# Another table of places for the loads, scatters and first expert loads of an attention with experts behind it

## The chip, the cores and the metric

The kernel runs on one core of a Trainium2 chip. The metric is the time of one execution in device microseconds, the median of several runs. TensorE is called PE, VectorE DVE, ScalarE ACT, GpSimd POOL and SyncE SP.

## The reference

Eight batches of eight heads, 576 positions, head size 64. Half of the heads see a local window of 32 positions, the other half the positions of the same remainder modulo 32. The heads' outputs are the tokens of a mixture of eight experts, of which each token takes one.

```python
scores = scale * np.matmul(q, k.transpose(0, 1, 3, 2))
masks = np.stack([mask_local if h < H // 2 else mask_strided for h in range(H)], axis=0)
scores = np.where(masks[None, :, :, :], scores, -1000000000.0)
attn = softmax(scores)
x = (attn @ v).transpose(0, 2, 1, 3).reshape(B * S, H * D)
...
logits = x @ w_gate + modality_bias[modality_id]
e_idx = np.argmax(logits, axis=1)
...
h = np.maximum(x[mask] @ w1[e], 0.0)
out[mask] = gate_w[mask, None] * (h @ w2[e])
```

(`softmax(scores)` stands for the reference's maximum, exponential and division.)

## The kernel before, in words

The attention is cut into 32 units, taken alternately from the local heads (class `Local`, L356 on) and the strided heads (class `Strided`, L459 on); each works on two batches or two heads at once. Four batch pairs, `bp` 0 to 3, have eight units each. A unit has five stages: its two loads of queries and keys (a and b, each 64 partitions, L354), its values (v and w, L371 and L473; a strided unit has v alone), `masks` (L379, L478), `scores` (`s` at L391 and L398, `ss` at L485, with the maximum, the subtraction and the exponential on DVE and ACT), `turn` (the transposes `t` and `ts`, L236) and `values` (`o` at L439 and L447, `oa` at L535, `ob` at L542, whose results DVE or ACT writes to the tokens `xa`, `xb` and `xc`). The main loop over n, 0 to 34, interleaves them: scores of unit n, turn of unit n-2, masks of unit n+1, values of unit n-3. Between them stand five places: 0 ahead of the scores, 1 behind them, 2 behind turn, 3 behind masks, 4 behind values. PE runs exactly in the order in which this code is written; on the other engines a scheduler orders what isn't pinned.

`FETCH[(n, place)]` names the loads that are issued at a place, as "20a" for unit 20, part a. All loads are issued by SP, in order, and each gets a wait on the last PE instruction written ahead of it:

```python
def paced(ins):
    behind(ins, next(i for i in reversed(nc.cur_bb.bb.instructions) if i.engine == mybir.EngineType.PE).name)
```

`SPOTS[n]` names the places at which `slot(n, place)` issues one further thing: a scatter of 128 finished tokens to their expert's region in DRAM (`xd`, L680, issued by POOL, nine for each batch pair), or, when the scatters of the first two pairs have been issued, the next step of `early()` (L1143 on; ten steps): the first expert's weights (`raw` in halves, then `lqk`, which serves as weight buffer again, L902) and the first two blocks of its tokens (`fx` in halves, L861). For n of 32 and up a missing entry means places 1, 2 and 4.

```python
def slot(n, place):

    if place not in SPOTS.get(n, (1, 2, 4) if n >= nu else ()):
        return
    if calm and not (todo and todo[0].args[0] < NBP - 2):
        next(calm[0], None)
        ...
    else:
        scatter_rows(1)
```

When a pair's units are done, `finish_pair` and `route` (L556 and L606 on) turn its tokens both ways, compute the gate (`lg`), the expert of each token and its row there. The rows of a pair are `posi` (L677, DVE), which the scatters read; one buffer is used for all pairs, so `posi` of a pair waits until the scatters of the pair before have landed. The token loads `fx` of the first expert wait for all scatters of the first two pairs (`collected`, L307 on). `turn_tokens` transposes these tokens on PE (`xt`, L236) behind the last unit's turn; then the experts run (`h` at L1052, `o` at L1070) to the end, with the routing of the last pair between their first steps.

Of the kernel before, what the change touches and what calls it, by code (L numbers as in the profile page):

```python
# [38 lines left out]
POPF = (2, 2)  # L39
LT, RK = 3, (13, 6)  # L40
SPOTS = {
    15: (2, 3, 4,), 16: (0, 1,), 18: (1,), 19: (2, 3, 4,), 23: (2, 3,), 25: (1, 2, 3,), 27: (2, 3, 4,), 28: (0,),
    29: (1, 2, 4,), 30: (0, 1,), 31: (1, 2, 4,),
}
FETCH = {
# [9 lines left out]
}  # L55
LAG = 2
FIRST, SECOND, SPLIT, SEND, GATHER, FAR = 1, 3, 4, 6, 7, 6
# [1296 lines left out]
```

## Time and profile before

| | us |
|---|---|
| median of 3 runs | 573.81 |
| the runs | 571.62 to 575.9 |
| the profiled execution | 577.81 |
| its span, first to last instruction | 575.7 |

A profile's span is cut by engines: PE (matmuls) and PEld (their weight loads) run beside each other, and a matmul shows as one row on each. "issue" is time in which an engine waited for nothing that the profile shows. SP's row of a load is the time of its issue, not of the transfer. The queue "instruction" moves program code, q1 the loads issued by SP, q0 the scatters issued by POOL.

### The profile page before, as it was taken

How to read it: one execution, taken by the hardware profiler on the slowest of the kernel's cores; microseconds unless marked ns; L12 is line 12 of the kernel's file. 1: busy time of each engine (PE TensorE's matmuls, PEld its weight loads, DVE VectorE, ACT ScalarE, POOL GpSimd, SP SyncE). 2: the span in 40 equal slices, each digit the busy share in tenths (PEclk: the TensorE clock that was granted, in tenths of full speed). 3: DMA queues.
4: the chain of work that ended last, by engine and by line, in shares of the span. 5: the costliest groups of instructions: out<-in, count | busy, mean ns of one | idle time of the engine just before them, and what ended most of it. 6: DMA issues, size and time to landing. Idle time of an engine off the chain costs nothing.

```text
span 575.7 us, 13499 instructions
## 1 busy us (share of the span) xinstructions
PE 546.1 (95%) x5273; PEld 463.0 (80%) x5273; DVE 378.6 (66%) x940; ACT 312.2 (54%) x651; POOL 89.0 (15%) x108
## 2 busy tenths in 40 slices
PE   6888798898999999999999999999999999999995
PEld 3677687776888999899888888888888888889984
DVE  7886877868977996777875626735734634547541
ACT  3476586676776666666643344343353353356642
POOL 2020212320603511011010020020020020021320
PEclk9899999998999999999999999999999999999998
DMA  8888988989999999998996672582482543455621
GB/s 290 271 287 295 309 279 285 303 313 370 389 322 282 317 367 347 356 304 233 309 248 245 141 266 78 147 275 91 128 253 95 153 178 111 128 202 174 246 92 40
DMA packets 65942, 137.00 MB, mean 238 GB/s; under 512 B 40383, under 2 KB 40767, under 8 KB 58816
## 3 DMA queue, kind: packets, MB, share of 16 engines
q1 hardware_dynamic: 59168, 112.46, 61.1%
q0 software_dynamic: 6416, 23.37, 11.0%
q8 instruction: 43, 0.70, 0.5%
q10 hardware_dynamic: 288, 0.24, 0.1%
q14 instruction: 27, 0.22, 0.1%
HBM read 107.97 MB, written 24.30 MB: 230 GB/s over the span
## 4 chain that ended last, share of the span: by engine, by line
PE 86%; issue 4%; DVE 4%; ACT 3%; DMA 1%; POOL 0%; SPq 0%; POOLq 0%; DVEq 0%; ACTq 0%
PE h L1052 35%; PE o L1070 35%; PE o L439 2%; PE oa L535 2%; PE s L391 2%; PE lg L612 1%; PE xl L236 1%; PE t L236 1%; PE xs L236 1%; PE ss L485 1%; ACT xc L548 1%; DMA lqk<-in_qkl 1%; PE ts L236 1%; PE s L379 1%; DVE mx L404 0%
## 5 line engine op out<-in xcount | busy, mean ns | idle before, releaser
L1052 PE MATMUL h<-xh,wh 128*128 128x256 f32 (+1 forms) x408 | 133.0, 326 | 0.1
L1052 PE MATMUL h<-xh,wl 128*128 128x256 f32 (+1 forms) x408 | 132.8, 326 | 0.0
L1052 PE MATMUL h<-xl,wh 128*128 128x256 f32 (+1 forms) x408 | 132.6, 326 | 0.0
L1070 PE MATMUL o<-wh,h 128*128 128x512 f32 x320 | 105.8, 392 | 0.0
L1097 DVE TENSOR_TENSOR wl<-lqk,wh 128x512 fp32r<-128x512 f32 x104 | 67.9, 687 | 54.2 <-ACT wh L1094 52.0
L1094 ACT CAST wh<-raw 128x512 fp32r<-128x512 f32 x102 | 58.6, 621 | 61.6 <-PE o L1070 57.8
L1078 POOL DMA_INDIRECT out<-y,le x36 | 39.0, 1083 | 326.8 <-ACT y L1077 320.2
L1097 DVE TENSOR_TENSOR wl<-raw,wh 128x512 fp32r<-128x512 f32 x102 | 66.4, 687 | 35.0 <-ACT wh L1094 34.9
L1094 ACT CAST wh<-lqk 128x512 fp32r<-128x512 f32 x104 | 59.9, 619 | 49.2 <-PE o L1070 49.2
L1052 PEld LDWEIGHTS h<-xh,wh 128*128 128x128 f32 x408 | 77.3, 189 | 9.6 <-ACT wh L1094 0.3
L1052 PEld LDWEIGHTS h<-xl,wh 128*128 128x128 f32 x408 | 77.3, 189 | 9.1
L1052 PEld LDWEIGHTS h<-xh,wl 128*128 128x128 f32 x408 | 77.3, 189 | 7.7 <-issue 0.4
L1070 PEld LDWEIGHTS o<-wh,h 128*128 128x128 f32 x320 | 60.1, 188 | 13.6
L1070 PE MATMUL o<-wl,h 128*128 128x512 f32 x160 | 62.9, 393 | 0.0
L1061 DVE SCALAR_TENSOR_TENSOR h<-h,h 128x512 fp32r<-128x512 f32 x40 | 27.7, 691 | 47.3 <-ACT h L1060 47.3
L1060 ACT ACTIVATE h<-h 128x512 fp32r<-128x512 f32 x40 | 23.9, 598 | 50.2 <-PE h L1052 50.1
L1070 PE MATMUL o<-wh,hh 128*128 128x512 f32 x128 | 51.1, 399 | 0.0
L1070 PE MATMUL o<-wl,hh 128*128 128x512 f32 x128 | 50.5, 395 | 0.0
L1070 PE MATMUL o<-wh,hl 128*128 128x512 f32 x128 | 49.1, 393 | 0.0
L1060 ACT ACTIVATE hh<-h 128x256 fp32r<-128x256 f32 x64 | 24.6, 385 | 20.2 <-PE h L1052 19.8
L1070 PEld LDWEIGHTS o<-wl,h 128*128 128x128 f32 x160 | 30.0, 188 | 6.7
L1061 DVE SCALAR_TENSOR_TENSOR hl<-h,hh 128x256 fp32r<-128x256 f32 x64 | 26.7, 417 | 5.5 <-ACT hh L1060 5.4
(211 smaller groups left out, 841.7 us busy)
## 6 DMA issues: line engine op xcount, KB each, us to landing
lqk<-in_w SPq DMA_DIRECT2D x26, 1024.0 KB, 9.7
raw<-in_w SPq DMA_DIRECT2D x24, 1024.0 KB, 5.2
lqk<-in_qkl SPq DMA_DIRECT2D x32, 296.0 KB, 4.8
vv<-in_vl SPq DMA_DIRECT2D x32, 292.5 KB, 6.3
sqk<-in_qks SPq DMA_DIRECT2D x32, 288.0 KB, 6.0
fx<-xd SPq DMA_DIRECT2D x16, 528.0 KB, 3.9
vs<-in_vs SPq DMA_DIRECT2D x16, 320.0 KB, 5.3
xd<-in_nul SPq DMA_DIRECT2D x9, 528.0 KB, 9.4
```

The lines of the kernel that those rows point to most:

```text
L236: nc.tensor.transpose(dst, src, ident)
L379: nc.tensor.matmul(sp, identb, cb[:, M_L + 64 * half:M_L + 64 * half + 64 * gn], start=True, stop=True)
L391: nc.tensor.matmul(sp[32 * u:32 * u + 32, 128 * m:128 * m + 128], q[:, i, :], kd[:, :, i:i + 2, :], start=False, stop=True, skip_group_che ...
L439: nc.tensor.matmul(o[64 * jj:64 * jj + 64, k, :], et[:, 2 * (k // 2) + bb, 2 * (k % 2) + jj, :, :].rearrange("p g q -> p (g q)"), vv[:, 4 ...
L535: nc.tensor.matmul(oa[64 * h:64 * h + 64, 126 * u:126 * u + 126], vs[0:126, 2 * u + h, :], eb[0:126, 4 * h + u, :, :].rearrange("p t q -> ...
L1052: nc.tensor.matmul(hp, wx[:, a1], x[:, c, :], start=(k == 0), stop=(k == 11))
L1060: evicted[f] = nc.scalar.activation(hh[:], hp, AF.Relu)
L1061: nc.vector.scalar_tensor_tensor(hl[:], hp, 0.0, hh.bitcast(F32), ALU.max, ALU.subtract)
L1070: nc.tensor.matmul(os[h], hx[:, m], w[:, 512:1024], start=(f == 0 and i == 0), stop=(f == 7 and i == 2))
L1078: outs.add(nc.gpsimd.indirect_dma_start(out, IOA(ap=le[:, 0:1], axis=0), y[:], None, bounds_check=NT - 1, oob_is_err=False))
L1094: ins = nc.scalar.copy(wh[:, c], raw[:, c])
L1097: nc.vector.tensor_tensor(wl[:, c], raw[:, c], wh[:, c].bitcast(F32), ALU.subtract)
```

## The change

Both tables are replaced; nothing else is. (Three more lines of table shift all later line numbers by 3.) `SPOTS` in full and two lines of `FETCH`:

```diff
 SPOTS = {
-    15: (2, 3, 4,), 16: (0, 1,), 18: (1,), 19: (2, 3, 4,), 23: (2, 3,), 25: (1, 2, 3,), 27: (2, 3, 4,), 28: (0,),
-    29: (1, 2, 4,), 30: (0, 1,), 31: (1, 2, 4,),
+    16: (0, 1, 4,), 17: (4,), 18: (0,), 20: (0, 1,), 22: (0, 4,), 25: (2, 4,), 26: (2, 4,), 27: (0, 4,), 30: (1, 2,),
+    31: (0, 1, 2,), 32: (0, 1, 2, 4,), 33: (1, 2,), 34: (0, 1,),
 }
 FETCH = {
...
-    (21, 1): "24a 24b 21v 25a", (22, 1): "25b 22v 22w 26a 26b", (23, 1): "27a", (23, 3): "23v 27b", (24, 0): "24v",
...
+    (21, 2): "25b", (21, 3): "20v 25a", (22, 0): "20w", (22, 1): "24a", (22, 2): "22v", (23, 0): "21v",
+    (23, 2): "23v", (23, 3): "26a", (24, 0): "26b 22w", (24, 2): "24v", (25, 0): "27a 27b 28a", (25, 2): "24w",
...
 }
```

The first place is on SP in loops 22 to 25, in the middle of the attention. `lqk` and `sqk` are queries and keys of local and strided units, `vv` and `vs` their values; the number is the buffer's. Before:

```order
L354 DMA sqk_85<-in_qks 64x1152 x2
L371 DMA vv_2051<-in_vl 64x1170 x2
L354 DMA lqk_84<-in_qkl 64x1184 x2
L354 DMA sqk_86<-in_qks 64x1152
L473 DMA vs_2195<-in_vs 128x640
L354 DMA sqk_86<-in_qks 64x1152
L371 DMA vv_2227<-in_vl 64x1170 x2
L354 DMA lqk_83<-in_qkl 64x1184 x2
L473 DMA vs_2332<-in_vs 128x640
```

Now:

```order
L357 DMA lqk_83<-in_qkl 64x1184
L374 DMA vv_2070<-in_vl 64x1170
L476 DMA vs_2089<-in_vs 128x640
L476 DMA vs_2186<-in_vs 128x640
L357 DMA lqk_84<-in_qkl 64x1184 x2
L374 DMA vv_2070<-in_vl 64x1170
L374 DMA vv_2264<-in_vl 64x1170
L357 DMA sqk_86<-in_qks 64x1152 x2
L357 DMA lqk_83<-in_qkl 64x1184
L374 DMA vv_2264<-in_vl 64x1170
L357 DMA sqk_85<-in_qks 64x1152 x2
```

From place (22, 1) to (24, 0) there were nine loads, the second `sqk_85` to the first `vv_2227`, at places with five, one, two and one; now there are seven, `lqk_83` to the second `vv_2070`, at places with one each but the last, which has two. PE's block of code that starts at 101.84 in the trace starts behind place (23, 3).

The second place is on SP at the end of the attention, loops 29 to 32: `raw` is the first expert's weights, `fx` its tokens, `vv_2811` and `vv_2792` the last local unit's values, `vs_2885` and `vs_2909` those of unit 31, `vs_2911` those of unit 29. Before:

```order
L371 DMA vv_2613<-in_vl 64x1170
L891 TENSOR_LOAD eb_2172
L902 ISA
L902 DMA raw_2759<-in_w 128x1024
L902 ISA
L902 DMA raw_2759<-in_w 128x1024
L856 TENSOR_LOAD row_2167
L861 ISA
L861 DMA fx_00_2809<-xd 128x528
L371 DMA vv_2811<-in_vl 64x1170 x2
L861 ISA
L861 DMA fx_00_2809<-xd 128x528
```

Now:

```order
L374 DMA vv_2792<-in_vl 64x1170 x2
L476 DMA vs_2909<-in_vs 128x640
L476 DMA vs_2911<-in_vs 128x640
L894 TENSOR_LOAD eb_2168
L905 ISA
L905 DMA raw_2919<-in_w 128x1024
L905 ISA
L905 DMA raw_2919<-in_w 128x1024
L859 TENSOR_LOAD row_2163
L864 ISA
L864 DMA fx_00_2965<-xd 128x528
```

The weights and tokens of the first expert now stand behind all of the attention's loads, of which the last, `vs_2909` and `vs_2911`, wait for the scores of unit 31 (`ss15`).

The third place is on DVE, loops 31 and 32: `posi` of the third pair, among the softmax of strided units (`sms`, `ens`, `tr`, `mxs`, `exs`) and the end of unit 28 (`rs`, `xa`, `xb`). Before:

```order
L676 TENSOR_REDUCE pos_2860<-po_2859 128x9
L507 TENSOR_TENSOR ens_2751<-exs_2744,sms_2747 128x288
L677 SCALAR_TENSOR_TENSOR posi_2861<-m_2668,pos_2860 128x9
L516 STREAM_TRANSPOSE tr_2934<-ens_2751 128x64
L495 TENSOR_REDUCE mxs_2919<-ss_2869 128x16
L526 TENSOR_TENSOR ec_2937<-tr_2934,cf_sb 128x144
L521 TENSOR_TENSOR eb_2936<-ts_2931,cf_sb 126x8x72
L498 TENSOR_TENSOR exs_2921<-ss_2869,mxs_2919 128x8x2x18
L452 TENSOR_SCALAR rs_2955<-o_2944 128x5
```

Now:

```order
L510 TENSOR_TENSOR ens_2745<-exs_2738,sms_2741 128x288
L519 STREAM_TRANSPOSE tr_2927<-ens_2745 128x64
L498 TENSOR_REDUCE mxs_2898<-ss_2848 128x16
L529 TENSOR_TENSOR ec_2930<-tr_2927,cf_sb 128x144
L524 TENSOR_TENSOR eb_2929<-ts_2924,cf_sb 126x8x72
L501 TENSOR_TENSOR exs_2900<-ss_2848,mxs_2898 128x8x2x18
L455 TENSOR_SCALAR rs_2948<-o_2937 128x5
L455 TENSOR_SCALAR rs_2961<-o_2952 128x4
L680 SCALAR_TENSOR_TENSOR posi_2839<-m_2661,pos_2838 128x9
L456 RECIPROCAL rs_2948<-rs_2948 128x5
L456 RECIPROCAL rs_2961<-rs_2961 128x4
L457 TENSOR_TENSOR xa_138<-o_2937,rs_2948 128x5x64
```

`posi` moved from behind the first `ens` to behind the two `rs` of unit 28. The last scatter of the second pair, for which it waits, moved from place (28, 0) to (31, 0).

## Rows read from the trace of the kernel before

**Rows 1.** The page, part 4: the chain that ended last, by engine.

```profile
PE 86%; issue 4%; DVE 4%; ACT 3%; DMA 1%; POOL 0%; SPq 0%; POOLq 0%; DVEq 0%; ACTq 0%
```

**Rows 2.** The chain in 0:165 us: start us, us, what.

```profile
25.05 1.70 issue
...
58.08 1.04 ACT xc L548
...
106.45 2.08 issue
...
119.04 1.17 issue
...
123.76 0.49 DVE xa L454
```

**Rows 3.** PE's waits in 0:160 us: us in total, times, longest.

```profile
PE ss L485 <- issue: 3.7, 3, 2.1
PE s L391 <- issue: 3.6, 4, 1.7
PE o L439 <- issue: 3.5, 2, 1.9
```

**Rows 4.** Stretches between PE's pauses: busy us and instructions (x) by engine, clock, DMA.

```profile
108.53:113.12 4.59, 4.59 (x125) 4.22 (x127) 3.86 (x19) 2.98 (x8) 2.67 (x3) 1.00 0.89 288
26.75:32.82 6.07, 4.48 (x126) 3.64 (x126) 4.67 (x14) 4.62 (x12) 0.00 (x0) 1.00 0.95 322
```

**Rows 5.** DMA queues in 101.84:106.1: packets, MB, share of 16 engines.

```profile
q1 hardware_dynamic: 307, 1.07, 83.9%
q14 instruction: 1, 0.01, 2.5%
q0 software_dynamic: 1, 0.00, 0.2%
```

**Rows 6.** DMA queues in 106.1:107.4, the code's queue.

```profile
q8 instruction: 1, 0.02, 5.4%
```

**Rows 7.** SP's queue in 96:108.6 in order of time: start us, us.

```profile
99.61 1.87 SPq L354 DMA_DIRECT2D lqk<-in_qkl  x2
101.58 0.54 SPq L354 DMA_DIRECT2D sqk<-in_qks  x1
102.22 0.53 SPq L473 DMA_DIRECT2D vs<-in_vs  x1
```

**Rows 8.** Stretches of 5 us, columns as in rows 4.

```profile
60.00:65.00 5.00, 3.67 (x121) 2.94 (x113) 5.00 (x23) 4.18 (x12) 0.00 (x0) 1.00 0.92 311
65.00:70.00 5.00, 2.98 (x68) 2.62 (x72) 3.01 (x12) 1.77 (x7) 2.71 (x3) 0.96 0.91 335
70.00:75.00 5.00, 5.00 (x115) 4.26 (x108) 3.69 (x13) 2.97 (x8) 2.33 (x3) 0.70 0.85 269
130.00:135.00 5.00, 4.33 (x139) 3.52 (x135) 4.95 (x22) 3.63 (x11) 0.00 (x0) 1.00 0.96 321
```

**Rows 9.** PE in 128:147 in order of time: start us, us.

```profile
133.60 0.31 PE L542 MATMUL ob<-ec,vs 128*64 128x72 f32 x4
...
140.46 1.46 PE L535 MATMUL oa<-eb,vs 126*64 126x126 f32 x16
...
143.54 1.09 PE L236 MATMUL xt<-cf_sb,fx 128*128 128x128 f32 x8
```

**Rows 10.** DVE in 130:146 in order of time.

```profile
139.31 0.16 DVE L452 TENSOR_SCALAR rs<-o 128x4 f32<-128x4 f32 x1 [0.60 <-PE o L439]
```

**Rows 11.** DMA issues in 120:150: KB each, median us to landing.

```profile
vv<-in_vl SPq DMA_DIRECT2D x4, 292.5 KB, 6.4
...
xd<-xb,posi POOLq DMA_INDIRECT x5, 6.5
xd<-xa,posi POOLq DMA_INDIRECT x5, 8.1
```

**Rows 12.** The page, part 6: the token loads.

```profile
fx<-xd SPq DMA_DIRECT2D x16, 528.0 KB, 3.9
```

18 rows, old and new, of the table FETCH are left out of this document.

## The prediction

> **What bounds the kernel now.** I read the page's chain first, then the chain of the first 165 us, then PE's waits there, then single stretches of PE, SP's queue and the DMA, then the last microseconds of the attention.
>
> PE carries 86% of the chain that ends last [rows 1]. From about 146 us on, PE works through the experts without a gap, and the change touches nothing there. What can move is the attention, where the chain leaves PE for two reasons. The first is called "issue": PE stands still though no data is late, 1.70 us at 25.05 and 2.08 us at 106.45 [rows 2]. The second is DVE with ACT: three stretches of the chain run on them alone, the first entered at 58.08, the last at 123.76 [rows 2]; DVE is busy 5.00 of 5 us in 60:65 and 4.95 of 5 in 130:135 [rows 8].
>
> What is "issue"? PE's own waits show it in every kind of matmul: 3.7 us ahead of `ss`, 3.6 ahead of `s`, 3.5 ahead of `o`, 10.8 us in nine pauses for these three alone [rows 3]. The pause at 106.45 falls inside one group of 64 equal matmuls, so no operand can be the cause. From the end of one pause (26.75) to the end of the next (32.82) there are 126 + 126 rows on PE and its weight loads, from 108.53 on another 125 + 127 in 4.59 us [rows 4]. So pauses come at multiples of some 252 instructions. I read that as PE running out of code: a queue called "instruction" moves one packet of 16 KB per such block. Between 101.84, where a block starts, and 106.1 no such packet moves while q1, the loads, moves 307 [rows 5]; it comes only in 106.1:107.4 [rows 6], and PE goes on at 108.53. In the 4 us ahead, SP had issued two `lqk` halves, one `sqk` and one `vs`, among others [rows 7], some 0.3 MB each. So I take it that a block's code is asked for when the block before it starts, and waits in the DMA line behind the loads that are there. That is what the new table must act on.
>
> **The change part by part.** The same loads, scatters and expert loads are issued; no instruction is added on PE, and PE's order in the attention is the same. Each load only waits for another PE instruction.
>
> *Pauses.* I put each load where its wait on PE stands in the program, and counted for each start of a block how many loads stand in the nine tenths of a block ahead of it. Before, 10 of 22 starts have six or more; after, 6. The ten carried 11.3 us of pauses, 1.13 each; the twelve others 4.1 us, 0.34 each (15.4 us in all from 20 us on, of which the eight that lie on the chain, 25.05 to 119.04, make 11.0 [rows 2]). With 6 and 16 it would be 6 x 1.13 + 16 x 0.34 = 12.2 us, 3.2 less. The place shown on SP is one: around the start at 101.84 nine loads stood in four bunches, now seven in ones and twos.
> What is gained this way is not all kept. Each of the three stretches on DVE and ACT cuts a lead back, since a PE that comes earlier finds DVE still busy; it is only the lead after the last of them that counts. I take half, **-1.5 us**. Bounds: 0, if the lead is cut entirely, and -11.0, if all eight pauses on the chain go and DVE follows.
>
> *The tail.* Here the table moves work later. The ninth scatter of the second batch pair stood at the start of unit loop 28; it now stands at the start of loop 31, behind the matmuls `ob` that start at 133.60 and end at 133.9 [rows 9]. A scatter takes 6.5 us to landing there [rows 11], so it lands near 140.4. Two things wait for it.
> DVE: `posi` of the third pair overwrites what the scatters read. It now stands right behind the two `rs`, the later of which runs at 139.31 [rows 10]; DVE stands there from 139.4 to 140.4, 1.0 us. Queued behind it are the normalising of unit 28 and the whole softmax tail of unit 31, which PE needs for its last `ts` and `oa`.
> SP: the first token load `fx` waits for all scatters of the first two pairs. Its two halves issue at about 140.8 and 141.2 and take 3.9 us [rows 12], so the second lands near 145.1. PE transposes those tokens at 143.54 [rows 9]: 1.6 us late. It lies beside DVE's delay, not on top.
> The last values (31v, 29v) move behind `ss15`, which ends at 134.6. The second issues near 135.2 and by 6.4 us for such a load [rows 11] lands at 141.6, against its use at 140.46 [rows 9]: 1.1 us, beside the others again. The first expert's weights also move behind `ss15`. Its first half megabyte, issued near 136, lands by 142.4 at those 6.4 us, and is used only behind the token transposes, which end at 144.6 [rows 9]; the other parts are used step by step after it. I cost that at nothing; the cover is some 2 us of PE's own work, and without it the first expert starts late by what is missing.
> The three together: **+1.8 us**. Bounds: 0 (the scatter lands in 5 us) and +5.6 (8.1 us to landing, as five others there [rows 11], is 1.6 more, and a token load that takes 6.4 in place of 3.9 is 2.5 more, on the 1.5 of DVE and SP).
>
> *Clock.* After a stretch with 2.98 busy us of 5 the granted clock fell to 0.70 for 70:75 [rows 8], between the two levels of 1.2 and 2.4 GHz; that costs 0.30 x 5 = 1.5 us of PE's work. One such fall may go with its pause or come in the tail: 0, bounds -1.5 and +1.5.
>
> Sum: -1.5 + 1.8 + 0 = +0.3 us. The profiled execution took 577.81 us (575.7 of span and 2.1 around it), so 578.1 for its like. It is 4.0 us above the median of the runs, 573.81, and nothing in these terms scales with that: 573.81 + 0.3 = **574.1 us**.
>
> One rule speaks against my reading of the pauses. The Trainium skill, "DMA: Bandwidth & Descriptors", section "Queues, rings and completion order", says that each DMA engine goes round the queues that have work, packet by packet. By it the code's packet would not stand behind the loads: it would take its turn at once, and no place of a load would matter. The 307 packets of q1 in the 4.3 us without one of the code's [rows 5] speak against it here, though no row shows the moment at which the code was asked for.
>
> **The rivals.** One per cent, 5.7 us, is about what a measurement of this kernel tells from no change.
> 1. The pauses on the chain all go and DVE keeps up: -11.0 + 1.8, **564.6 us**. For it: DVE is at 3.01 of 5 in 65:70 [rows 8] and could start earlier there. Against it: its full stretches [rows 8], and six starts that still have many loads ahead. 0.17.
> 2. Slower: the late scatter sets the end of the attention. Place: `posi` on DVE and `fx` on SP in loop 32. Price: the upper bound of 5.6 us and a fall of the clock, 1.5, with no lead to set against it: 580.9, by the sums above; **580 us**. It decides from the point where scatter and tokens together take over 14 us from 133.9. Against it: the line has fewer attention loads by then. 0.16.
> 3. The pauses don't depend on the loads' places (the code is late for another reason, or takes its turn anyway): 0 + 1.8, **575.6 us**. 0.12.
> 4. The change doesn't do what it says: SP issues in order and is often behind its waits, so the loads go out when they did. Then neither term comes: **573.8 us**. Against it: bunches of five to seven loads are split over several places. 0.05.
>
> **How the numbers follow.** My forecast has 0.50, with its own range 570.5 to 578: the pauses between 0 and -4.5, the tail between 0 and 4, the clock to either side. Faster by over 1% (under 568.1) is rival 1: 0.17. Slower by over 1% (over 579.5) is rival 2: 0.16. The rest, 0.50 + 0.12 + 0.05 = 0.67, is within 1%. The range of 8 in 10 goes part of the way to the outer rivals: 567.8 to 580.4.
>
> **What would show it right or wrong.** Right: "issue" on PE's lines before 135 us falls by 3 us or more, most of it at 106 and 119; waits on DVE ahead of `ts` grow; the chain shows DVE `posi`, a scatter or `fx` between 135 and 146; the first matmul of the experts starts within 2 us of where it did. Wrong: if "issue" nearly goes and the experts start over 5 us earlier, DVE was no bound; if "issue" stays, my reading of the code's wait is wrong; if PE stands for over 4 us at the token transposes, I took the tail too low.

## The result, and the profile after

The changed kernel takes **581.96 us** (median, 577.3 to 585.57), the kernel before 575.84 beside it: ratio **1.0118**, 95% interval 1.0094 to 1.0141. (A ratio leaves out, on both sides, the slow executions, those over 1.5% above the fastest of their kernel, so it is not the quotient of the two medians.) The forecast was 574.1 us in a range up to 580.4. The profiled execution took 584.14 us, against 577.81 before.

The first lines are the page's chain by engine, which answers to [rows 1].

```profile
PE 76%; DMA 12%; DVE 5%; issue 4%; SPq 1%; ACT 1%; POOL 1%; POOLq 0%; DVEq 0%
```

DMA had 1% of the chain and has 12%. The chain that ended last, between 131 and 155 us (start us, us, what; it answers to [rows 2] at the end of the attention):

```profile
131.24 1.62 issue
...
134.21 0.96 POOL xd L683
...
135.47 0.96 POOL xd L683
...
136.74 7.14 DMA xd<-xb,posi
...
143.96 0.18 DVE posi L680
...
144.18 1.60 PE oa L538 x16
...
147.63 7.20 DMA fx<-xd
```

The chain leaves PE at 134, runs over three scatters on POOL, the landing of the last one, `posi` on DVE, `oa` on PE, and the token loads `fx`.

PE at the end of the attention, with the idle time ahead of an instruction and its releaser in brackets (it answers to [rows 9]):

```profile
135.69 0.29 PE L545 MATMUL ob<-ec,vs 128*64 128x72 f32 x4
...
138.83 0.77 PE L239 MATMUL t<-cf_sb,ex 128*128 128x128 f32 x5
144.18 1.58 PE L538 MATMUL oa<-eb,vs 126*64 126x126 f32 x16 [4.59 <-DVE posi L680]
...
149.31 1.97 PE L239 MATMUL xt<-cf_sb,fx 128*128 128x128 f32 x8
```

PE stands 4.59 us ahead of `oa`, from 139.59 on. DVE at the same place (it answers to [rows 10]) stands 4.82 us ahead of `posi`:

```profile
138.93 0.22 DVE L455 TENSOR_SCALAR rs<-o 128x5 f32<-128x5 f32 x2
143.96 0.17 DVE L680 SCALAR_TENSOR_TENSOR posi<-m,pos 128x9 int32<-128x9 f32 x1 [4.82 <-DMA xd<-xb,posi]
```

The profile puts PE's stand down to `posi`, and so the chain runs through it. But `oa` reads `eb` and `vs`, not `posi`, and its wait includes the signals of the second load of `vs`, the values of unit 29 (29v). SP issued this load late, at 137.36, as the second of these two:

```profile
136.97 0.81 SPq L476 DMA_DIRECT2D vs<-in_vs  x2
...
138.55 1.29 SPq L905 DMA_DIRECT2D raw<-in_w  x2
```

In the trace the last of its signals comes at 144.05, 6.7 us after the issue, and `posi` ends at 144.13. The two ended together by chance. That PE need not wait for `posi` there is shown by x6b below, where `oa` runs 4 us ahead of a late `posi`; what the late `posi` holds is `ts`, two steps on.

Stretches of 5 us (busy us and instructions by engine, granted clock, DMA share; they answer to [rows 8]):

```profile
140.00:145.00 5.00, 0.82 (x12) 0.85 (x14) 1.04 (x5) 1.44 (x4) 0.00 (x0) 0.96 0.94 358
145.00:150.00 5.00, 4.43 (x53) 3.80 (x50) 3.94 (x14) 2.07 (x5) 0.00 (x0) 0.50 0.88 229
150.00:155.00 5.00, 5.00 (x49) 4.55 (x48) 3.81 (x10) 4.53 (x9) 2.23 (x3) 0.86 1.00 384
```

In 140:145 PE is busy for 0.82 us, and in the 5 us behind it the granted clock is 0.50, which is 1.2 GHz, the lower of its two levels. So the stand is paid twice: the same 16 `oa` take 1.58 us at 144.18 where they took 1.08 at 127.11.

What became of the pauses shows in PE's waits from 34 to 127 us (us in total, times, longest us), which answer to [rows 3]; the six longest:

```profile
PE o L442 <- DMA vv<-in_vl: 1.4, 1, 1.4
PE s L394 <- issue: 1.4, 1, 1.4
PE ss L488 <- issue: 1.3, 2, 1.0
PE s L401 <- issue: 0.9, 1, 0.9
PE t L239 <- ACT xa L566: 0.7, 1, 0.7
PE s L394 <- DMA lqk<-in_qkl: 0.7, 1, 0.7
```

Over all its lines "issue" makes 3.8 us, waits for data and other engines 4.5, 8.3 together. In the same stretch of the kernel before there was 9.6 us of "issue" and 1.4 of `ts` on DVE, 11.0 together. In a second profile of it (run x16 below) it was less; the five longest:

```profile
PE s L391 <- issue: 2.7, 1, 2.7
PE s L398 <- issue: 1.6, 1, 1.6
PE o L439 <- issue: 1.5, 1, 1.5
PE ss L485 <- issue: 1.4, 1, 1.4
PE ts L236 <- DVE posi L677: 1.2, 1, 1.2
```

That is 7.2 of "issue" and 1.4 of the rest.

To compare kernels by stretch I took the same instruction in each, since PE's order is the same in all: rows of PE and its weight loads in order of start, counted from 0. Row 1193 is near 33 us, 5209 near 127, 5962 near 145 (the last `oa` ahead of the experts).

| kernel | start of row 1193 | to 5209 | to 5962 | profiled time |
|---|---|---|---|---|
| before | 32.8 | 93.9 | 18.7 | 577.81 |
| before, second profile (x16) | 33.2 | 94.8 | 18.9 | 578.87 |
| after | 33.2 | 94.2 | 24.8 | 584.14 |
| x1 | 29.9 | 93.8 | 25.7 | 581.89 |
| x2 | 30.6 | 96.5 | 19.3 | 579.01 |
| x3 | 33.1 | 93.5 | 22.8 | 580.22 |
| x4 | 33.4 | 92.6 | 23.9 | 580.99 |
| x5b | 35.0 | 90.9 | 20.9 | 578.77 |
| x6b | 34.0 | 94.3 | 23.5 | 583.51 |
| x7b | 31.1 | 94.2 | 23.7 | 581.46 |
| x9 | 32.4 | 92.8 | 20.6 | 578.23 |

Up to 127 us the changed kernel stands between the two profiles of the kernel before. The whole difference, 24.8 - 18.8 = 6.0 us, comes in the last stretch. Behind row 5962 the three need the same time to within 0.4 us. The last stretch itself (us; PE runs the same 381 matmuls in each):

| kernel | PE stands | PE busy | granted clock |
|---|---|---|---|
| before | 2.71 | 15.96 | 0.91 |
| before, second profile (x16) | 4.36 | 14.56 | 1.00 |
| after | 7.39 | 17.38 | 0.86 |

So 3.0 to 4.7 us of the difference are standing, and 1.4 to 2.9 us are the same work at a lower clock.

### The profile page after: what moved, and what is told of

Its sections match the earlier page's. It is cut to its first block, busy times and chain, and to the rows that moved or that the text cites. A ratio compares the mean times of both kernels' runs of the same rounds, so it can differ in the third digit from the quotient of the medians.

```text
span 582.2 us, 13526 instructions
## 1 busy us (share of the span) xinstructions
PE 549.5 (94%) x5273; PEld 464.9 (80%) x5273; DVE 376.4 (65%) x940; ACT 310.9 (53%) x651; POOL 94.1 (16%) x108
## 4 chain that ended last, share of the span: by engine, by line
PE 76%; DMA 12%; DVE 5%; issue 4%; SPq 1%; ACT 1%; POOL 1%; POOLq 0%; DVEq 0%
PE o L1073 31%; PE h L1055 31%; DMA cols<-rows 5%; PE o L442 3%; PE s L394 2%; DMA vv<-in_vl 2%; PE oa L538 2%; DMA lqk<-in_qkl 2%; PE ss L488 1%; DMA xd<-xa,posi 1%; DMA fx<-xd 1%; DMA xd<-xb,posi 1%; PE t L239 1%; PE xs L239 1%; DVE wl L1100 1%
## 5 line engine op out<-in xcount | busy, mean ns | idle before, releaser
L1081 POOL DMA_INDIRECT out<-y,le x36 | 42.6, 1184 | 318.8 <-ACT y L1080 312.8
L1100 DVE TENSOR_TENSOR wl<-raw,wh 128x512 fp32r<-128x512 f32 x102 | 66.1, 688 | 33.1 <-ACT wh L1097 33.1
L1063 ACT ACTIVATE h<-h 128x512 fp32r<-128x512 f32 x40 | 23.9, 598 | 49.1 <-PE h L1055 49.1
```

The costliest lines, as they stand in the source:

```text
L1063: evicted[f] = nc.scalar.activation(hh[:], hp, AF.Relu)
L1081: outs.add(nc.gpsimd.indirect_dma_start(out, IOA(ap=le[:, 0:1], axis=0), y[:], None, bounds_check=NT - 1, oob_is_err=False))
L1100: nc.vector.tensor_tensor(wl[:, c], raw[:, c], wh[:, c].bitcast(F32), ALU.subtract)
```

## The experiments

Three theories stood at first. A: the late scatters hold `posi` and the tokens, and that is the loss. B: the new places of the loads cost the time. C: the loads gain and the scatters lose more.

**x1, x2: one table at a time.** x1 has the loads as changed and `SPOTS` as before, x2 the reverse.

```diff
-SPOTS = { 16: (0, 1, 4,), ... 34: (0, 1,) }
+SPOTS = { 15: (2, 3, 4,), ... 31: (1, 2, 4,) }
```

> The changed kernel with the load table as changed and the table of scatters and first expert loads as before. Theory A (the loss is the late scatters alone, which hold `posi` on DVE and the token loads on SP; the new places of the loads are worth about nothing): 575 to 577 us, within 0.4% of the kernel before, and PE stands under 1 us ahead of the last `oa` groups. Theory B (the new places of the loads cost the time: values and keys that now come late take the place of the pauses): 580 to 583 us. Theory C (the new loads gain some 2 us and the scatters lose 8): 573 to 574 us.

> The changed kernel with the load table as before and the table of scatters and first expert loads as changed. Theory A: 581 to 583 us, with the same stand of 3 to 5 us on PE ahead of `oa` while `posi` waits for the scatters of the second pair. Theory B: 575 to 577 us. Theory C: 583 to 585 us.

Measured: x1 583.33 us, ratio 1.0119 (1.0082 to 1.0156), as slow as both together; x2 579.32, 1.0063 (1.0024 to 1.0103). All three theories fall: A, because x1 is slow without the late scatters; B, because x2 lies above before; C, because x1 gains nothing. PE's longest wait of x1 from 127 to 153 us names something else:

```profile
PE oa L538 <- DMA vs<-in_vs: 4.0, 1, 4.0
```

`oa` waits for the values of unit 29 (29v), which the new load table issues at (31, 1) in place of (29, 0). With the old `SPOTS` they stand behind three halves of the first expert's weights, issued from 127.10 to 132.81: issued at 134.58, they land at 142.8 and hold PE until 142.9. In x2, `posi` waits 0.8 us: the same three scatters, at the same places, land nearly in time when the loads are the old ones. (By the number alone x1 is 0.3 us outside theory B, and x2 lies between the theories.)

**x3, x4: one late thing mended.** x3 issues the three scatters in loop 28, x4 gives `posi` a second buffer.

```diff
-    27: (0, 4,), 30: (1, 2,), 31: (0, 1, 2,),
+    27: (0, 4,), 28: (0, 1, 2,), 31: (1, 2,),
...
-        posi = ap.tile([P, 9], I32, tag="posi", name=f"posi{bp}")
+        posi = ap.tile([P, 9], I32, tag="posi", bufs=2, name=f"posi{bp}")
```

> The changed kernel with the last three scatters of the second pair issued in loop 28 (places 0, 1, 2) in place of loops 30 and 31; the expert loads stay where the change put them. Theory A: the three land by about 132, `posi` does not wait, the tokens are there when PE transposes them: 575 to 577 us. Rival D (what costs is the expert loads and tokens behind them, moved three loops later, not the scatters): 580 us or more, with PE standing at the token transposes `xt`. Theory B: 581 to 583 us.

> The changed kernel with a second buffer for `posi`, so that DVE need not wait for the scatters; all places as changed. If DVE's wait alone is the price: 576 to 577.5 us. If the tokens, which wait for the same scatters on SP, end just as late beside it: the stand of 4.6 us ahead of `oa` goes, PE then stands 2 to 4 us at the token transposes, and the time is 579 to 581.5 us. If neither matters (theory B): 581 to 583 us.

Measured: x3 581.85 us, 1.0115 (1.0083 to 1.0147); x4 582.23, 1.0117 (1.0063 to 1.0171). Neither gives anything back against the changed kernel's 1.0118. PE in x4, where `posi` does not hold DVE:

```profile
142.69 1.95 PE L538 MATMUL oa<-eb,vs 126*64 126x126 f32 x16 [4.02 <-DMA vs<-in_vs]
```

and PE's two longest waits of x3 from 135 to 153 us:

```profile
PE xt L239 <- DMA fx<-xd: 2.4, 2, 1.9
PE oa L538 <- DMA vs<-in_vs: 1.0, 1, 1.0
```

Each repair uncovers the next late thing. New theory: 29v, `posi` and the tokens are late side by side, and only what mends all three mends the tail.

**x5 to x7: the values.** x7 moves 29v and 31v alone in the kernel before, x6 moves them back in the changed kernel, x5 does that and has the old `SPOTS`.

```diff
# x6, and x5 with SPOTS of before
-    (29, 0): "28v", (30, 0): "28w 30v", (30, 3): "30w", (31, 1): "31v 29v",
+    (29, 0): "28v 29v", (30, 0): "28w 30v", (30, 3): "30w", (31, 0): "31v",
# x7, in the kernel before
-    (29, 0): "29v 28w", (30, 0): "30v 30w", (31, 0): "31v",
+    (29, 0): "28w", (30, 0): "30v 30w", (31, 1): "31v 29v",
```

> The changed kernel with only the last values back: 29v at (29, 0), 31v at (31, 0); late scatters as changed. Theory A2 (three things are late side by side, 29v, `posi` and the tokens, so mending one brings little): 579 to 582 us, PE standing 2 to 5 us at `oa` for `posi` or at the token transposes. If 29v alone is the price: 575 to 577 us.

> The kernel before with one load moved: 29v (and 31v beside it) to (31, 1), where the change has them; all else as before. Theory A: `oa` of unit 29 waits 3 to 5 us for its values, which stand behind the first expert's weights in the DMA line: 579 to 583 us. Theory B: 575 to 577 us.

The expectation of x5 was 573 to 577 us if the late values are what the new loads cost, 580 to 583 if it is the other loads. In this set of runs the kernel before took 591.59 us. Medians and ratios: x7 594.49, 1.0082 (1.0043 to 1.0121); x6 587.54, 0.9953 (0.9915 to 0.9991); x5 596.35, 1.0100 (1.0049 to 1.0152). Since x6 came out faster than before and x5 slower, all three were measured once more, on another chip (before 576.87).

> The changed kernel with only the last values back, once more, beside the kernel before on another chip. If `posi` and the tokens hold the tail as long as 29v did (theory A2): 0.6 to 1.2% slower than before. If 29v alone was the price: within 0.4% of before, and the stand of 4.6 us ahead of `oa` is gone while PE waits under 3 us at the token transposes. In the first look it was 0.5% faster than before, on a chip on which the kernel before took 591.6 us.

> The kernel before with 29v and 31v moved to (31, 1), once more. Theory A: `oa` of unit 29 waits 3 to 4 us for its values and the time is 0.5 to 1.2% longer than before. Theory B: no difference.

> The changed kernel's loads with the scatters and expert loads of before and the last values back (29v at (29, 0), 31v at (31, 0)), once more, beside the kernel before on another chip. Theory A (29v behind the expert weights is what the new load table costs when the scatters stand as before): within 0.5% of the kernel before, no stand of PE over 1.5 us at `oa` after 130 us. Theory B (the new places of the other loads cost the time): 1% slower, as in the first look at this kernel.

Measured: x7b 580.94, ratio 1.0076 (1.0050 to 1.0102): one load moved by two loops, and one by a place, cost 0.8%, 4 to 5 us, in both sets alike. x6b 580.26, 1.0062 (1.0025 to 1.0099): about half of the loss is gone, and what holds the tail now is `posi`, as theory A2 had it. PE and DVE in x6b:

```profile
140.86 1.08 PE L538 MATMUL oa<-eb,vs 126*64 126x126 f32 x16
...
145.28 0.17 DVE L680 SCALAR_TENSOR_TENSOR posi<-m,pos 128x9 int32<-128x9 f32 x1 [3.56 <-issue]
...
146.46 0.66 PE L239 MATMUL ts<-cf_sb,ens 128*126 128x128 f32 x2 [4.38 <-DVE ens L510]
```

(The profile names no cause for DVE's wait; in the trace the last signal of the third late scatter, issued at 137.69, comes at 145.20.) x5b 578.84, 1.0053 (1.0017 to 1.0090), with no stand at `oa` at all: between the two theories of its expectation, and no decision for either.

**x8: does code wait behind loads?** In the kernel before, six of the nine loads ahead of the block that starts near 102 us move behind it.

```diff
-    (22, 1): "25b 22v 22w 26a 26b", (23, 1): "27a", (23, 3): "23v 27b", (24, 0): "24v",
+    (22, 1): "25b 22v 22w", (24, 2): "26a 26b 27a 27b 23v", (24, 3): "24v",
```

> The kernel before with the loads ahead of one block of PE's code thinned: of the nine that stood in the block before the one that starts near 102 us, six (26a 26b 27a 27b 23v 24v) move half a block behind it. If the code waits behind the loads that are in the line: its packet starts within 2.5 us of the block's start in place of 4.3, the pause that was 2.08 us at 106.45 falls under 0.5, and the pause at the next block's start, near 113, grows from none to 0.5 to 2. If the code is late for another reason: a pause of 1 to 2 us stays at 106. The time is 575 to 577 us either way, since one pause is traded for another.

x7 ran beside it in the same set with the table of before at this place, so the two are compared. The block started at 104.29 in x7. Its DMA queues in 104.2:108.9 (packets, MB, share):

```profile
q1 hardware_dynamic: 393, 1.26, 70.8%
...
q8 instruction: 1, 0.02, 1.3%
```

The code's packet began to move at 107.82, 3.5 us behind the block's start. In x8 the block started at 106.68, and in 106.6:108.4 there was

```profile
q1 hardware_dynamic: 9, 0.03, 3.9%
q8 instruction: 1, 0.02, 3.4%
```

with the packet at 107.34, 0.66 us behind. So at this start the code came late where loads filled the line and early where they did not. At the next start, where the loads now stand in x8, it is the other way, 2.2 us in x8 and 1.0 in x7. The other traces agree, with a wide spread: over 18 starts in each of the 20 kept traces the packet begins 1.2 us behind the start (median of 26) where the DMA engines were under half busy in the first 0.6 us, and 2.5 us (median of 290) where they were over 0.8 busy. That the code is asked for at the start of the block is still an assumption; no row shows it. Neither kernel paused at the ends of these two blocks, so what an early packet is worth was not seen, and the time, 592.25 us, 1.0042 (1.0007 to 1.0077), shows no gain.

**x9: all three mended.** 29v and 31v back as in x6, the scatters in loop 28, the expert loads from (30, 1) on.

```diff
-    27: (0, 4,), 30: (1, 2,), 31: (0, 1, 2,),
+    27: (0, 4,), 28: (0, 1, 2,), 30: (1, 2,), 31: (0, 1, 2,),
```

> The changed kernel with all three late things of the tail moved earlier: 29v at (29, 0), 31v at (31, 0), the last three scatters of the second pair in loop 28, the ten expert loads from (30, 1) on. If the tail's three late things are the whole loss (theory A): 573 to 576.5 us on a chip where the kernel before takes 575.8, with PE standing under 1.5 us each at `oa` and at the token transposes. Theory B (the loads in the middle cost it): 580 us or more.

Measured: 580.14 us, ratio 1.0061 (1.0026 to 1.0095). PE's waits from 135 to 153 us, where the changed kernel stood 4.6 us at once:

```profile
PE ts L239 <- DVE ec L529: 1.4, 1, 1.4
PE xt L239 <- DMA fx<-xd: 0.9, 2, 0.6
PE ts L239 <- DVE ens L510: 0.8, 1, 0.8
```

The last stretch falls from 24.8 to 20.6 us, the clock stays at 1.00, and the profiled time, 578.23, lies between those of the two profiles of before. So the stand in the tail comes from the three late things. The loss as a whole is not explained by it: the stands are those of theory A, but the median is the one that theory B asked for (580 us or more), 3.3 us over before, and about half of the changed kernel's 1.2% is left, if a ratio of 1.0061 tells anything (see x16). Where these 3.3 us lie the profile, of one execution, does not show.

**x10, x11, x13, x15: is there something to gain?** x10 takes the changed places for units 9 to 18 alone, x11 those for units 0 to 8, both in the kernel before. x13 and x15 move only the expert loads. x14 has the changes of x10 and x13 together; it was expected at a ratio of 0.993 to 0.995 if both were gains.

```diff
# x13
-    29: (1, 2, 4,), 30: (0, 1,), 31: (1, 2, 4,),
+    29: (4,), 30: (0, 1, 2,), 31: (0, 1, 2, 4,),
# x15
-    29: (1, 2, 4,), 30: (0, 1,), 31: (1, 2, 4,),
+    30: (1, 2, 4,), 31: (0, 1, 2, 4,), 32: (0, 1, 4,),
```

> The kernel before with the changed places for the loads of units 9 to 18 alone. In the profiles so far the stretch from 33 to 80 us of PE's code (blocks 4 to 12) took 44.2 to 45.7 us with the changed loads and 46.3 to 47.7 with those of before, while all that came ahead of it and behind it was slower with the changed table. If that part is a gain of its own: 1.5 to 2 us faster than before (ratio 0.9965 to 0.9975). If a lead gained there is cut back behind it by DVE, as the prediction had it: no difference (ratio 0.998 to 1.002).

> The kernel before with the changed places for the loads of units 0 to 8 alone. If the changed first loads come late (PE stood 0.3 to 1.1 us for `sqk` at 27 to 30 us in every profile with them, and in none without): 1 to 2 us slower than before (ratio 1.002 to 1.0035). If that is made good behind it: no difference.

> The kernel before with the ten expert loads issued two places later, so that no expert weights stand ahead of the code of the block that starts near 134 us. If the pause of 2.4 to 2.9 us there (in all profiles with the scatters and expert loads of before) is the code behind those weights: it falls under 1 us, the first matmul of the experts comes 1 to 2 us earlier, ratio 0.996 to 0.998. If it is DVE's (the matmul waits for `ec`): the pause stays, ratio 1.0. If the weights' delay is what counts: PE stands at the first expert's matmuls and the ratio is over 1.002.

> The kernel before with the ten expert loads from (30, 1) on, so that the first weights are issued behind the start of the block of PE's code that starts near 131 us, not ahead of it. If the pause at the next block's start (2.4 to 2.9 us in every profile with the old places of the weights) is code waiting behind those weights: the packet starts within 2.5 us of the block's start in place of 4.0, the pause falls under 1 us, and the time is 0 to 2 us under the kernel before (ratio 0.9965 to 1.0). If it is DVE's `ec`: the pause stays at 2 us or more.

Measured: x10 579.93 us, 1.0068 (1.0031 to 1.0106); x11 582.77, 1.0102 (1.0060 to 1.0145); x13 578.34, 1.0045 (1.0019 to 1.0071); x14 579.95, 1.0030 (0.9992 to 1.0069); x15 576.49, 0.9982 (0.9945 to 1.0020). None is faster. In x10 "issue" is 6.0 us where the two profiles of before have 9.6 and 7.2, and a late value load and waits on ACT come in its place (PE's waits from 34 to 127 us):

```profile
PE ss L524 <- issue: 3.6, 2, 1.9
PE o L478 <- DMA vv<-in_vl: 2.5, 1, 2.5
```

In x11 a value load at the seam between the two tables comes late (24 to 60 us):

```profile
PE o L484 <- DMA vv<-in_vl: 3.0, 1, 3.0
```

Mixing two tables makes a third line of loads with late ones of its own, so these two say little about the changed table's parts. x13 was no test: the first weights still went out at 130.15 (130.06 before), and the pause stayed at 2.5 us. x15 moved the weights to 135.20, behind the block's start at 133.87; the pause was 1.36 us and the packet came 2.9 us behind the start. But the second profile of the unchanged kernel has 1.1 us and 2.5 us there, so x15 decides nothing.

**x16: the kernel before beside itself.**

> The kernel before, unchanged, beside itself. It shows what a ratio of two sets of runs of one kernel gives, and a second profile of it. Expected: 0.998 to 1.002; if it lies outside, ratios of 1.003 to 1.006 of the other kernels tell nothing. For the stretches of PE's code in the profile: 46 to 48 us from block 4 to 12, 46.4 to 47.3 from 12 to 20, 7.7 to 8.3 from 20 to 22, 10 to 11 from 22 to 23.

Measured: 575.97 us, 0.9975 (0.9940 to 1.0010). That is just outside the 0.998 to 1.002 of the expectation, by which ratios of 1.003 to 1.006 tell nothing: those of x13, x14 and x5b fall there, and x2, x6b, x9 and x10 lie at its edge. x1, x3, x4, x11 and the change itself are well outside, and x7 is outside in two sets. The kernel was set beside itself in this last set of runs alone; how far the ratios of the other sets can be off as a whole is not known.

## Why the prediction was wrong

Of the 7.9 us between the forecast of 574.1 and the 581.96 measured, 2.0 are its base: it stood on the median of three runs, 573.81, and beside the changed kernel the same kernel took 575.84. The rest, 5.8 us, is the change itself: +0.3 was forecast and +6.1 measured.

**The pauses (-1.5).** The signal I had asked for came: on the chain "issue" from 20 to 135 us fell from 11.0 us in eight parts to 6.8 in five (1.78, 1.42, 1.04, 0.91 and 1.62), and the pauses at 106 and 119 went; on PE's lines before 135 us it fell from 14.5 to 8.7. The gain did not come: to row 5209 the changed kernel needs 94.2 us, before 93.9 and 94.8. What went in "issue" came back as late values and keys (1.4 and 0.7 us) and waits on ACT and DVE (2.4). My half was too much, and my lower bound of 0 was right. The second profile of before shows a further fault: the pause at 119 is not there, another stands at 113.7 (1.6 us), and the one at 96 is 2.7 in place of 1.3. I priced single pauses of one profile as if they belonged to the table. My reading of their cause is supported by x8 and not proved.

The Trainium skill, "DMA: Bandwidth & Descriptors", section "Queues, rings and completion order", has each engine go round its queues packet by packet. In x7 and x8 the code's packet begins 3.5 us behind the block's start with 393 packets of loads in between and 0.66 us with 9; if it is asked for at the start, it does not get its turn at once here. The Trainium skill, "Runtime: NRT & Kernel Launch", section "Instruction fetch mechanics", calls the fetch of the next 16 KiB mostly hidden. The "issue" of 7.2 and 9.6 us between 34 and 127 us in the two profiles of before says, if it is the code, that it is not hidden for this PE program.

**The tail (+1.8).** This is the term that failed: +6.0 us by the table. Its three parts stood in the prediction, rightly as things side by side, and each was too small. The step that failed is the moment at which PE and DVE come to need the late things. I took it from the rows of the one profile of before, and in these PE stands ahead of `ts`, just behind `ob`:

```profile
137.04 0.44 PE L236 MATMUL ts<-cf_sb,ens 128*126 128x128 f32 x2 [2.44 <-DVE ec L526]
```

and has a granted clock of 0.79 in 135:140. The changed kernel stands 0.61 us there, and the second profile of before 1.11. So PE was ready for the `oa` of unit 29 6.5 us behind the end of `ob` in my rows (140.46 against 133.91), but 3.6 us behind it in the changed kernel (139.59 against 135.98) and 4.1 in x16. The landings, counted from the end of `ob`, I had to within 0.4 us for 29v and 1.4 us for the last scatter and the tokens.
- *29v, 1.1 us; measured 4.0 in x4,* where `posi` does not hold DVE, and 4.6 in the changed kernel. Forecast to land 7.7 us behind `ob`, it landed 8.1 behind it (144.05), and 7.4 in x4. So nearly all of the miss is PE's earlier arrival. The move costs 0.76% by itself (x7b), and I had laid it beside the others as the least of the three.
- *`posi`, 1.0 us; measured 4.8.* DVE comes to it at 139.15, 3.2 us behind `ob` in place of 5.5: 2.3 us. The landing adds 1.4, 7.9 us behind `ob` in place of 6.5: I counted one scatter, and three were waiting. POOL's rows start at 134.21, 135.47 and 136.74, since two more stand at (30, 1) and (30, 2) and POOL takes 1.27 us for each; and the last took 7.14 us to landing in place of 6.5.
- *The tokens, 1.6 us; measured 2.4 in x3,* where the other two hold PE for 1.0 us only. In the changed kernel itself they held nothing: the second half landed at 148.46, and PE came to `xt` at 149.31.

**The clock (0).** The fall to 0.50 in 145:150 goes with the stand: x6b, with a stand of 4.4 us, has 0.50 too, and x9, without one, 1.00. I had it as a chance of 1.5 us to either side, not as part of a stand's price. By the table of the last stretch it makes 1.4 us against the first profile of before, whose own stand of 2.44 us is followed by 0.79 and 0.87, and 2.9 us against the second, which stays at 1.00.

**The signs.** The chain shows `posi`, a scatter and `fx`, as I had it. The first matmul of the experts starts 6.7 us later (152.45 against 145.71), not within 2. The stand of over 4 us came, at `oa` and not at the token transposes.

**The rivals.** Rival 2 came nearest: slower by 6.1 us, where its sum of tail and clock has 7.1; I gave it 0.16. Of its place `posi` is right; 29v, which held PE at `oa` and costs 0.76% alone, it does not name, and `fx` did not hold PE in the changed kernel. My argument against it, that the line has fewer attention loads by then, fails in the row 140:145, where the DMA share is 0.94: the weights of the first expert, issued from 138.55 on, are in the line. Its stated point, scatter and tokens over 14 us from 133.9, was passed in the trace with 14.6 (148.46), in a profile in which `ob` ends 2.1 us later than in my rows. Rival 1 and rival 4 are out. Rival 3 has x8 against it as a mechanism, but half of its arithmetic, no gain from the pauses, is what happened.

**What stays open.** Why x2, x5b and x9 have ratios of 1.005 to 1.006 while their profiled runs (579.01, 578.77 and 578.23) are about even with the two of before (577.81 and 578.87): x9 leaves half of the loss, and whether that half is the loads in the middle or an offset of the set of runs is not known. And what the changed places of the middle loads are worth by themselves, since x10 and x11 made lines of their own.

## What to carry to other kernels

Where several things are made later at one place, price each against the moment at which its user will come to it in the changed kernel, with the pauses taken out that the old profile happens to have there, and against the queue that it really stands in: what is ahead of it on the issuing engine and in the DMA line. Expect that mending one alone brings nothing. A stand of PE of some 4 us is to be priced with the clock behind it, here 1.4 to 2.9 us beside 3.0 to 4.7 of standing. Where the profile names one cause of a wait, compare it with what the waiting instruction reads: here two things ended within 0.1 us, and the one named was not the one that PE needed. Pauses read from one profile move by 1 to 2 us in the next one of the same kernel, so a search over places needs a second profile and, in the same set of runs, a comparison of the kernel with itself before a difference under 0.6% is believed.

## What the runs showed of the hardware

The kernel before took 575.8 to 576.9 us in five sets of runs and 591.6 in the one with x5 to x8. The record gives that set chip number 14, and gives the same number to the later set of x10 to x14, in which the kernel took 576.15; so the number does not tell the cause. In the set with 591.6 the first expert stood 6.0 us in the kernels with the old places of the expert loads (x7 and x8: PE `h` behind ACT's `wh`), and not in x6, which issues them later; ACT's chain in x7 shows, between its own instructions, time for which the profile finds no cause in this program:

```profile
156.41 3.32 another core or an unknown queue
...
160.34 2.22 another core or an unknown queue
```

So the sign of a change of places can turn from one set of runs to another: x6 was 0.9953 there and 1.0062 in the next. What ACT waited for was not tried.
